# A planned attention and expert kernel: the order of all its tasks is drawn anew, a small load of q moves from ScalarE's queue to GpSimd's, and nine idle products stand where six stood

## The chip, the cores and the metric

The kernel runs on one core of a Trainium2 chip. The metric is device time in microseconds (us) of one execution. It is the median of 3 runs for the kernel before, and one further execution was profiled. TensorE (PE) multiplies matrices and writes to PSUM; VectorE (DVE), ScalarE (ACT) and GpSimd (POOL) work on tiles in SBUF, the first two on PSUM as well; SyncE (SP) issues most transfers.

## The reference

```python
# q, k, v: (4, 8, 1152, 64) float32; w_in (512, 2048), w_out (2048, 512)
q_pool = q.reshape(B, H, S // 2, 2, D).mean(axis=3)
scores = np.matmul(q_pool, k.transpose(0, 1, 3, 2)) / np.sqrt(D)
attn = np.exp(scores - scores.max(-1, keepdims=True))
attn = attn / (attn.sum(-1, keepdims=True) + 1e-09)
x = np.matmul(attn, v).transpose(0, 2, 1, 3).reshape(B * S // 2, H * D)   # (2304, 512)
h = x @ w_in
g = np.where(h > 0, h, np.exp(np.minimum(h, 0)) - 1)
out = g @ w_out
```

## The kernel before

**Units and pairs.** There are four units, one for each batch entry. Each has four pairs of heads, and each pair nine score steps: four tiles of 128 pooled queries for each head, and one step that takes the last 64 queries of both heads. After attention a unit's 576 tokens go through the experts in two groups, of 256 and 320 tokens.

**A score step.** `scores` multiplies q by k into the one PSUM tile `s` (L935 and L941 in float32 for the first two pairs; L956, L961 and L970 in float16 halves for the others). `biggest` on DVE (L985) takes the scaled scores out of `s` into an `ep` tile with the row maximum, and only then can PE write the next scores. `expo` on ACT (L991) makes the exponentials. In the four pairs of the first unit and one later pair PE transposes them (L1067) and they are copied to `pT` (L1077 on ACT or L1080 on DVE); in the other pairs they are divided into a high and a low float16 half (L1036, L1042 or L499, then L1045 on DVE) and transposed by DMA. PE multiplies by v (L1101, L1119).

**Preparing a pair.** `prep` loads q, k and v. The first two pairs are plain: `q_twice` (L655) adds the two rows that are pooled, `flip_turn` (L624) transposes on PE and `flip_out` (L627) copies to `kT` and `qT`. For all later pairs `halves` makes the high half of q and k, and in eleven pairs of v (L676 on ACT, or L499) and then the low half, either on DVE in one pass over two tiles (L693), or on POOL in two passes (L499, then L699).

**Weights.** Thirty-two loads bring w_in and w_out (L805). Each is decoded by three DVE passes (L820, L821, L824; the last two read two tiles), then every 256 columns are split into halves: the high one on ACT (L847), DVE or POOL (L499), the low one on DVE (L850), or on POOL (L499, then L856).

**Experts.** L1229 is the first product and L1310 the second. Between them lie L1242 and L1245 on ACT, `em` on POOL (L1250), ACT (L1255) or DVE (L1260), the join L1265 on DVE, the high half (L1279 or L1287) and the low half (L1283 on POOL or L1291 on DVE). L1326 and L1329 take the result out.

**What sets the order.** Every step is a task added to a plan with the engines that may do it. The table `ORDER` lists all 2,691 tasks with an engine letter each (p, v, a, g, s: PE, DVE, ACT, POOL, SP), and `SLOTS` gives each buffer its place. The kernel emits tasks in that order, so each engine does its own in it; when something starts on the chip follows from the waits alone. The tables come from a search with a replay of the plan. Task costs (such as `Port(...)`, which marks a pass that shares GpSimd's port in the replay) served that search: what the chip executes depends on the tables and the task bodies only. `warm` multiplies the identity by itself into an unused PSUM tile (L760).

Of the kernel before, what the change touches and what calls it, by code (L numbers as in the profile page):

```python
# [32 lines left out]
2s 1s 11p 4a 16v 299s 9p 3a 314s 13v 5a 12a 10a 19v 17p 7p 283s 18a 414p 22s 288s 8a 301v 23s 316v  # L33
370s 294s 415v 14p 15a 427p 285v 20p 21a 428v 429a 0p 437p 435p 289s 431p 27p 34g 416a 31v 290v
319s 422p 438v 28a 404p 372v 32p 29p 439a 432a 423a 417g 405v 35p 25p 26a 406a 36a 291v 460p 461v
440g 441p 442a 321v 37g 42s 38p 40s 433p 30a 462a 434a 33a 450p 451v 443p 296v 418p 407g 436a 496p
497v 452a 419a 444a 293s 410p 420p 421a 45a 292a 39v 453g 458p 459v 408p 409a 6s 313s 309s 463v
411v 430g 41g 483p 484v 44a 359s 445p 446a 456p 468p 469a 304s 412p 473p 457a 295v 466p 474v 298s
498a 499g 467a 46p 447p 315v 47v 311v 413a 475a 519p 284s 448a 476v 297a 464p 454p 504p 48a 520v
449v 465a 49g 424p 485a 52a 300v 455a 505a 303s 509p 500p 510v 306v 481p 317a 487p 482a 502p 477p  # L40
555p 501a 50s 511a 488a 302a 503a 521a 470p 556v 478a 24s 55s 542p 479p 557a 480a 525p 471a 526a
308s 51s 318s 425a 506p 305v 286v 543v 515p 489p 507a 426v 508v 472v 486v 287a 490v 369s 532p 516a
307a 558g 559p 533v 522v 517p 523p 527p 491p 544a 524a 518a 565p 310v 56v 492a 493p 534a 53g 566v
371v 54s 59a 494a 567a 538p 578p 573p 560a 528a 513p 495v 569p 539a 574a 579v 57s 360s 550p 570a
320v 43s 375s 563p 561p 514a 562a 564a 551a 60a 601p 546p 571p 535g 568g 548p 536p 602v 61p 322a
361v 547a 364s 588p 512g 529p 572a 580a 62v 63a 67a 603a 589v 537a 530a 614p 64v 365s 377v 581v
615v 575p 531v 576v 312a 323v 577v 65s 70s 582p 605p 637p 590a 66s 545v 583a 604g 549a 606a 68g
638v 594p 607p 608a 609p 324p 584p 585a 610a 69s 616a 540p 647p 611p 366v 325v 541a 595a 648v 373a
596p 586p 618p 587a 326p 649a 367v 624p 552p 597a 327v 639a 625v 328g 683p 626a 612v 650v 591v 640v
# [36 lines left out]
1996v 1989v 1990g 1974g 1991g 1015v 2034p 1001v 986p 1008a 1016a 1003s 1024p 1009g 1975v 1010a
# [251 lines left out]
def attention_moe_kernel(  # L338
# [69 lines left out]
    def dve(n):  # L408
        return Port(1.08 * n + 75.0)
# [4 lines left out]
    def pol(n):  # L414
        return 0.93 * n + 150.0
# [968 lines left out]
```

## Time and profile before

| | |
|---|---|
| median of 3 runs (lowest, highest) | 743.45 us (743.11, 743.52) |
| the profiled execution | 742.65 us |
| its span, first to last instruction | 740.9 us |
| PE busy | 717.3 us, 97% of the span |
| DVE busy | 625.0 us, 84% |
| ACT busy | 560.6 us, 76% |
| POOL busy | 338.0 us, 46% |

The span is 1.75 us shorter than the execution that it belongs to, and that execution was 0.80 us faster than the median. Busy shares are means over stages with different limits, so the stages below count for more than the table. PE's busy time is the union of pipelined matmuls; it is not a share of its peak.

### The profile page before, as it was taken

What the parts mean: (1) busy time and instruction counts of PE and PEld (TensorE: products, weight loads), DVE (VectorE), ACT (ScalarE), POOL (GpSimd) and SP (SyncE); (2) the same over time, 40 slices, a digit from 0 to 9 for tenths busy, and PEclk for the clock granted to TensorE, in tenths of its full rate; (3) what the DMA queues carried; (4) which work ended last, traced back from release to release, by engine and by line L of the source; (5) the groups of instructions that cost most, each with busy time, mean ns of one, the idle gap of its engine ahead of it and who ended that gap; (6) DMA issues with size and microseconds to landing.
All of it is one profiled execution on the core that took longest, in us unless ns stands there. A gap on an engine that the chain in (4) does not pass through costs nothing.

```text
span 740.9 us, 19632 instructions
## 1 busy us (share of the span) xinstructions
PE 717.3 (97%) x7905; PEld 478.8 (65%) x7905; DVE 625.0 (84%) x1098; ACT 560.6 (76%) x974; POOL 338.0 (46%) x385
## 2 busy tenths in 40 slices
PE   5899998999999999999999999999999999999997
PEld 4577776877565555775676566786665665865753
DVE  6999999999998998879898879899988989875330
ACT  3899997998998887777688766889788564752651
POOL 1322455466626633376465554354646452440430
PEclk9999999999999999999999999999999999999999
DMA  8787834577999998999999999899899998793001
GB/s 304 287 228 251 247 119 105 142 135 160 171 179 207 178 204 169 211 181 174 213 171 208 189 205 181 163 162 209 173 189 194 188 162 137 139 139 64 30 1 36
DMA packets 310971, 126.01 MB, mean 170 GB/s; under 512 B 286304, under 2 KB 288352, under 8 KB 310880
## 3 DMA queue, kind: packets, MB, share of 16 engines
q1 hardware_dynamic: 310432, 124.16, 82.4%
q8 instruction: 62, 1.02, 0.6%
q10 hardware_dynamic: 448, 0.59, 0.2%
q14 instruction: 29, 0.24, 0.1%
HBM read 45.09 MB, written 4.72 MB: 67 GB/s over the span
## 4 chain that ended last, share of the span: by engine, by line
PE 47%; DVE 3%; ACT 2%; issue 1%; DVEq 0%; ACTq 0%
PE r L1310 16%; PE r L1229 14%; PE r L1119 6%; PE s L956 4%; PE s L970 3%; PE r L1101 1%; DVE ep L985 1%; PE r L1067 1%; ACT ep L991 1%; PE s L961 0%; DVE ep L1045 0%; DVE tmp L1265 0%; DVE x L1207 0%; DVE g L1291 0%; ACT hb L1042 0%
## 5 line engine op out<-in xcount | busy, mean ns | idle before, releaser
L991 ACT ACTIVATE ep<-ep,wk 128x1152 f32<-128x1152 f32 x136 | 170.4, 1254 | 45.7 <-DVE ep L985 40.5
L1229 PE MATMUL r<-x,wi 128*128 128x256 f16 (+1 forms) x1536 | 196.6, 286 | 1.5 <-DVE tmp L1265 1.5
L985 DVE TENSOR_SCALAR_CACHE_REDUCE ep<-s,sm 128x1152 f32<-128x1152 f32 x122 | 172.3, 1412 | 13.0 <-PE s L970 9.2
L1229 PEld LDWEIGHTS <-wi 128*128 128x128 f16 x1536 | 147.6, 98 | 43.6 <-issue 6.1
L1310 PE MATMUL r<-wo,g 128*128 128x512 f16 (+1 forms) x864 | 174.9, 380 | 0.1
L1045 DVE SCALAR_TENSOR_TENSOR ep<-ep,wk,hb 128x1152 f16<-128x1152 f32 x99 | 146.0, 1478 | 6.7 <-ACT hb L1042 4.7
L1310 PEld LDWEIGHTS <-g 128*128 128x128 f16 (+1 forms) x864 | 73.3, 100 | 83.8 <-issue 4.7
L956 PE MATMUL s<-kT,qT 128*128 128x512 f16 (+3 forms) x420 | 82.9, 328 | 4.3 <-DVE ep L985 3.3
L1119 PEld LDWEIGHTS <-v 128*64 128x64 f16 x2970 | 77.8, 110 | 11.4 <-issue 10.5
L1119 PE MATMUL r<-pT,v 128*64 128x128 f16 (+1 forms) x2970 | 84.4, 215 | 0.3 <-DVE tmp L1265 0.3
L1283 POOL TENSOR_TENSOR g<-tmp,g 128x320 f16<-128x320 f32 (+1 forms) x61 | 68.1, 1118 | 36.0 <-ACT g L1279 34.4
L499 POOL TENSOR_SCALAR wk<-wk 128x1 f32<-128x1 f32 x68 | 31.2, 459 | 114.3 <-ACT ep L991 93.9
L1042 ACT ACTIVATE hb<-ep,wk 128x1152 f16<-128x1152 f32 x50 | 62.3, 1249 | 17.3 <-POOL wk L1010 8.2
L1036 POOL TENSOR_SCALAR hb<-ep,wk 128x1152 f16<-128x1152 f32 x34 | 44.3, 1303 | 56.6 <-DVE wk L1001 29.6
L1265 DVE SCALAR_TENSOR_TENSOR tmp<-r,tmp 128x320 f32<-128x320 f32 (+1 forms) x96 | 51.5, 551 | 21.5 <-POOL tmp L1250 11.5
L1242 ACT ACTIVATE tmp<-r 128x320 f32<-128x320 f32 (+1 forms) x96 | 45.1, 480 | 23.0 <-PE r L1229 14.7
L1245 ACT ACTIVATE tmp<-tmp,us 128x320 f32<-128x320 f32 (+1 forms) x96 | 57.8, 610 | 2.0 <-DVE us L1184 0.5
L956 PEld LDWEIGHTS <-qT 128*128 128x128 f16 (+1 forms) x420 | 33.9, 100 | 37.4 <-issue 13.7
L970 PE MATMUL s<-kT,qT 64*128 64x512 f16 (+1 forms) x280 | 49.6, 391 | 0.9 <-DVE ep L985 0.9
L1077 ACT ACTIVATE pT<-r 128x384 f32<-128x384 f32 x96 | 43.7, 498 | 8.7 <-PE r L1067 8.4
L1067 PE MATMUL r<-ident,ep 128*128 128x128 f32 x333 | 47.3, 283 | 2.3 <-DVE x L1134 2.3
L1287 POOL TENSOR_SCALAR g<-tmp 128x320 f16<-128x320 f32 (+1 forms) x42 | 28.8, 686 | 39.5 <-DVE tmp L1265 39.5
(163 smaller groups left out, 1044.0 us busy)
## 6 DMA issues: line engine op xcount, KB each, us to landing
v<-in_v_dram SPq DMA_DIRECT2D x16, 576.0 KB, 4.3
k<-in_k_dram SPq DMA_DIRECT2D x15, 576.0 KB, 4.5
g<-in_moe_w_in_dram SPq DMA_DIRECT2D x15, 512.0 KB, 7.2
q<-in_q_dram SPq DMA_DIRECT2D x15, 512.0 KB, 4.3
g<-in_moe_w_out_dram SPq DMA_DIRECT2D x15, 512.0 KB, 5.4
out_dram<-tmp SPq DMA_DIRECT2D x16, 256.0 KB, 3.0
qT<-qT SPq DMA_DIRECT2D x28, 144.0 KB, 3.0
pT<-hb SPq DMA_TRANSPOSE x99, 3.6
```

The source lines that it names most:

```text
L956: nc.tensor.matmul(s.ap[rows, c, 0:n], pr.qT.ap[:, 1 - c % 2, j, rows], keys[h][c], start=first[c], stop=not first[c] and c < 2, skip_grou ...
L970: nc.tensor.matmul(s.ap[rows, c, 0:512], pr.qT.ap[r, c, j, rows], keys[h][c][r], start=first[c], stop=not first[c], skip_group_check=True,)
L985: nc.vector.tensor_scalar(e_(), s.ap.rearrange("p a b -> p (a b)")[:, 0:S], -0.5 / float(D) ** 0.5 if pr.plain else pr.sm.ap[:, 12:13], No ...
L991: nc.scalar.activation(out=e_(), in_=e_(), func=AF.Exp, bias=nm.ap[:, 0:1], scale=-1.0, accum_out=nm.ap[:, 1:2],)
L1042: nc.scalar.activation(out=hb.ap, in_=e_(), func=AF.Copy, scale=nm.ap[:, 1:2])
L1045: nc.vector.scalar_tensor_tensor(out=e16(), in0=e_(), scalar=nm.ap[:, 1:2], in1=hb.ap, op0=ALU.mult, op1=ALU.subtract)
L1067: nc.tensor.transpose(tp.ap[:, c * 128:(c + 1) * 128], e_()[:, (j + c) * 128:(j + c + 1) * 128], ident)
L1119: nc.tensor.matmul(half(h), pr.v16.ap[:, h, order[c], e], p, start=(j + c == 0), stop=(j == 2 and c == NCH - 1), skip_group_check=True,)
L1229: nc.tensor.matmul(hp.ap[:, f * n:(f + 1) * n], w_in16[g][:, a, c, (f0 + f) * 128:(f0 + f + 1) * 128], x16.ap[:, e, c, g0:g0 + n], start=( ...
L1245: nc.scalar.activation(out=en.ap[:, :m], in_=en.ap[:, :m], func=AF.Exp, scale=us.ap[:, 8:9])
L1283: nc.gpsimd.tensor_tensor(out=l, in0=gv, in1=h, op=ALU.subtract)
L1310: nc.tensor.matmul(op.ap[r0:r0 + tn, :], gt[qd].ap[:, a, fi, o:o + tn], w_out16(f // 2)[:, e, f % 2, :], start=(i < 128 // tn), stop=(i >= ...
```

## The change

Four things change. `load_qb`, two transfers of 32 KB for the first pair, is issued by GpSimd instead of ScalarE. `warm` makes nine products, not six. The cost of `halves`' low half of q and v becomes a `Port`, which no engine executes. And both tables are replaced. The diff, with one line of each table:

```diff
 ORDER = """
-2s 1s 11p 4a 16v 299s 9p 3a 314s 13v 5a 12a 10a 19v 17p 7p 283s 18a 414p 22s 288s 8a 301v 23s 316v
+4a 16v 299s 5g 19g 3a 2s 1s 9p 314s 10a 17p 283s 288s 13v 18a 301v 11p 12a 316v 14p 414p 415v 15a
...
 SLOTS = """
-01 00 00 00 03 00 01 00 00 04 00 02 00 00 00 01 00 01 04 04 00 01 01 03 03 00 00 02 00 00 00 02 00
+00 00 00 00 04 00 00 02 00 03 00 01 01 00 00 01 00 01 02 03 00 02 01 04 00 00 00 00 00 00 00 02 00
...
         def load_qb():
             for h in range(2):
-                nc.scalar.dma_start(
+                nc.gpsimd.dma_start(
...
-            tq.append(plan.add("ACT", 900.0, lk - 8.0, load_qb, (), [q32]))
+            tq.append(plan.add("POOL", 2000.0, lk - 8.0, load_qb, (), [q32]))
...
-            t = plan.add("DVE", Port(730.0, 730.0) if j == 1 else dve(n) + 35.0 * (j == 0), kl, f, [h], bufs, ...
+            t = plan.add("DVE", Port(730.0, 730.0) if j == 1 else Port(dve(n) + 35.0 * (j == 0)), kl, f, [h], bufs, ...
...
     def warm():
-        for i in range(6):
+        for i in range(9):
             nc.tensor.matmul(idle.ap[:, 0:128], ident, ident, start=True, stop=True)
...
-    plan.add("PE", 1530.0, -1.0e9, warm, [], [idle])
+    plan.add("PE", 2340.0, -1.0e9, warm, [], [idle])
```

**The start.** SP's queue before, from its first transfer (`k` and `q` are the inputs of the first pair, then of the second; `h` and `g` take raw weights):

```order
L600 DMA k_79<-in_k_dram 128x576 x2
L805 DMA h_88<-in_moe_w_in_dram 128x2x512
L805 DMA g_96<-in_moe_w_in_dram 128x2x512
L805 DMA g_115<-in_moe_w_in_dram 128x2x512
L558 DMA q_123<-in_q_dram 128x2x512
```

SP's queue of the changed kernel from the same place:

```order
L805 DMA h_83<-in_moe_w_in_dram 128x2x512
L600 DMA k_89<-in_k_dram 128x576 x2
L805 DMA g_97<-in_moe_w_in_dram 128x2x512
L805 DMA g_106<-in_moe_w_in_dram 128x2x512
L805 DMA g_108<-in_moe_w_in_dram 128x2x512
L558 DMA q_146<-in_q_dram 128x2x512
```

One weight load now stands ahead of the two loads of k, and a fourth ahead of the next pair's q. POOL's queue of the changed kernel where it makes the identity:

```order
masks.py:197 MEMSET ident 128x128
L593 DMA q_79<-in_q_dram 64x128
masks.py:199 ISA
masks.py:199 AFFINE_SELECT ident<-ident 128x128
L593 DMA q_79<-in_q_dram 64x128
L655 TENSOR_TENSOR kn_81<-q_79 128x128
```

Before, POOL held only the three rows of the identity here; the two L593 stood on ACT's queue and this L655 on DVE's, behind two others. The load q_146 on SP now waits for POOL's L655, which waits for the two L593.

**The splits of w_in.** POOL before, in the first unit, where it makes low halves of k (`kn`) and of w_in (`wi`):

```order
L499 TENSOR_SCALAR k_1117<-k_1117,sm_1139 128x1152
L699 TENSOR_TENSOR kn_1138<-k_1117,kn_1138 128x9x128
L499 TENSOR_SCALAR wk<-wk 128x1
L1013 TENSOR_TENSOR wk<-wk 128x1
L499 TENSOR_SCALAR wi_67<-wi_67,wk 128x1024
L856 TENSOR_TENSOR wi_66<-wi_67,wi_66 128x1024
```

DVE before, beside it:

```order
L985 TENSOR_SCALAR ep_1470,wk<-s_1440,sm_333 128x1152
L1140 COPY x_416<-r_1447 128x128
L1003 TENSOR_SCALAR wk<-wk 128x1
L1004 RECIPROCAL wk<-wk 128x1
L693 SCALAR_TENSOR_TENSOR qn_1214<-q_928,sm_1139,qn_1214 128x9x64
L1134 TENSOR_TENSOR x_416<-r_1447,x_416 128x128
L985 TENSOR_SCALAR ep_1512,wk<-s_1497,sm_333 128x1152
L820 TENSOR_SCALAR tmp_1514<-g_1242 128x512
L821 SCALAR_TENSOR_TENSOR tmp_1514<-g_1242,tmp_1514 128x512
L824 SCALAR_TENSOR_TENSOR wo_1284<-g_1242,tmp_1514 128x512
L1134 TENSOR_TENSOR x_416<-r_1518,x_416 128x128
```

POOL of the changed kernel in the same place:

```order
L699 TENSOR_TENSOR qn_1282<-q_984,qn_1282 128x9x64
L499 TENSOR_SCALAR wi_66<-wi_66,wk 128x1024
L856 TENSOR_TENSOR wi_65<-wi_66,wi_65 128x1024
L499 TENSOR_SCALAR k_1106<-k_1106,sm_1212 128x1152
L699 TENSOR_TENSOR kn_1211<-k_1106,kn_1211 128x9x128
L499 TENSOR_SCALAR wi_67<-wi_67,wk 128x1024
L856 TENSOR_TENSOR wi_66<-wi_67,wi_66 128x1024
```

DVE of the changed kernel beside it:

```order
L985 TENSOR_SCALAR ep_1465,wk<-s_1458,sm_372 128x1152
L1003 TENSOR_SCALAR wk<-wk 128x1
L1004 RECIPROCAL wk<-wk 128x1
L1171 TENSOR_REDUCE us_1473<-x_385 128x1
L985 TENSOR_SCALAR ep_1510,wk<-s_1497,sm_372 128x1152
L820 TENSOR_SCALAR tmp_1545<-g_1158 128x512
L821 SCALAR_TENSOR_TENSOR tmp_1545<-g_1158,tmp_1545 128x512
L824 SCALAR_TENSOR_TENSOR wo_1290<-g_1158,tmp_1545 128x512
L1134 TENSOR_TENSOR x_385<-r_1475,x_385 128x128
```

The low half of this pair's q (qn) has left DVE: POOL makes it by L499 and L699 ahead of the place shown. The decode passes L820, L821 and L824 still stand beside POOL's L499 and L856 on w_in.

**The last expert group.** DVE before, at the start of the last group of 320 tokens:

```order
L1207 SCALAR_TENSOR_TENSOR x_9758<-x_7928,us_10515,x_9758 128x4x320
L1184 TENSOR_SCALAR us_10515<-wk,us_10515 128x1
L499 TENSOR_SCALAR us_10515<-wk,us_10515 128x1 x2
L1265 SCALAR_TENSOR_TENSOR tmp_10646<-r_10632,tmp_10646 128x320
L1265 SCALAR_TENSOR_TENSOR tmp_10683<-r_10669,tmp_10683 128x320
```

DVE of the changed kernel there:

```order
L1207 SCALAR_TENSOR_TENSOR x_9757<-x_7946,us_10592,x_9757 128x4x320
L499 TENSOR_SCALAR us_10592<-wk,us_10592 128x1
L1260 TENSOR_SCALAR tmp_10663<-tmp_10663,us_10592 128x320
L1265 SCALAR_TENSOR_TENSOR tmp_10663<-r_10632,tmp_10663 128x320
L1260 TENSOR_SCALAR tmp_10711<-tmp_10711,us_10592 128x320
L1265 SCALAR_TENSOR_TENSOR tmp_10711<-r_10671,tmp_10711 128x320
```

More of the `em` passes stand on DVE. Over the whole program L1260 goes from 17 to 30, L1291 from 28 to 36 and L1131 from 19 to 30, L1140 from 9 to 2; on POOL L1283 goes from 68 to 60, L1036 from 34 to 28; on ACT L1255 from 47 to 36, L1128 from 36 to 25, L1137 from 16 to 23. PE has the same products but for the three idle ones.

## Rows read from the trace of the kernel before

**Rows 1.** Busy time in stretches (in us): length, engine's busy time (instructions), clock, DMA.

```profile
6.00:20.00 14.00, 12.02 (x61) 8.46 (x61) 12.22 (x20) 6.13 (x11) 2.02 (x3) 1.00 0.99 344
20.00:100.00 80.00, 77.74 (x805) 58.11 (x806) 77.34 (x165) 76.03 (x156) 28.32 (x37) 1.00 0.78 248
100.00:140.00 40.00, 36.48 (x420) 28.71 (x417) 38.62 (x72) 34.48 (x72) 23.12 (x22) 0.96 0.44 113
140.00:240.00 100.00, 96.46 (x1080) 65.88 (x1080) 95.95 (x168) 93.19 (x152) 52.81 (x49) 1.00 0.90 162
240.00:660.00 420.00, 417.70 (x4896) 272.56 (x4890) 372.05 (x618) 315.25 (x521) 212.46 (x242) 1.00 0.99 182
```

**Rows 2.** Timeline of DVE, 113 to 124 us: start, duration, instruction.

```profile
114.00 2.18 DVE L693 SCALAR_TENSOR_TENSOR qn<-q,sm,qn 128x576 f16<-128x576 f32 x1
...
118.10 1.40 DVE L821 SCALAR_TENSOR_TENSOR tmp<-g,tmp 128x512 uint32<-128x512 uint32 x1
119.54 2.50 DVE L824 SCALAR_TENSOR_TENSOR wo<-g,tmp 128x512 uint32<-128x512 uint32 x1
```

**Rows 3.** Timeline of POOL, 111 to 124 us.

```profile
113.19 2.38 POOL L699 TENSOR_TENSOR kn<-k,kn 128x1152 f16<-128x1152 f32 x1
...
117.61 1.36 POOL L499 TENSOR_SCALAR wi<-wi,wk 128x1024 f32<-128x1024 f32 x1 [0.75 <-ACT wi L847]
119.05 2.44 POOL L856 TENSOR_TENSOR wi<-wi,wi 128x1024 f16<-128x1024 f32 x1
```

**Rows 4.** Timeline of PE, 114 to 127 us; in brackets PE's idle time and who ended it.

```profile
122.39 0.52 PE L1067 MATMUL r<-ident,ep 128*128 128x128 f32 x3 [2.26 <-DVE x L1134]
123.63 0.94 PE L956 MATMUL s<-kT,qT 128*128 128x512 f16 x3 [0.72 <-DVE wo L985]
```

**Rows 5.** Busy time in a short stretch, columns as in rows 1.

```profile
123.80:127.30 3.50, 3.50 (x17) 2.55 (x15) 3.00 (x10) 0.65 (x3) 0.00 (x0) 0.51 0.90 200
```

**Rows 6.** The pass L693: ns shortest/median/longest, first and last start.

```profile
L693 DVE SCALAR_TENSOR_TENSOR qn<-q,sm,qn x11: 804/1115/2182, 72.5 to 577.5; 128x576 f16<-128x576 f32 x11
```

**Rows 7.** Timeline of PE, 5.5 to 17 us.

```profile
6.02 1.30 PE L624 MATMUL r<-ident,k 128*128 128x128 f32 x5 [6.02 <-DMA k<-in_k_dram]
...
10.83 0.56 PE L941 MATMUL s<-kT,qT 64*128 64x128 f32 x2
...
14.90 1.50 PE L760 MATMUL r<-ident 128*128 128x128 f32 x12
16.47 0.70 PE L935 MATMUL s<-kT,qT 64*128 64x512 f32 x2
```

**Rows 8.** Timeline of DVE, 4 to 14 us.

```profile
10.65 0.69 DVE L821 SCALAR_TENSOR_TENSOR tmp<-g,tmp 128x512 uint32<-128x512 uint32 x1
11.38 0.69 DVE L824 SCALAR_TENSOR_TENSOR wi<-g,tmp 128x512 uint32<-128x512 uint32 x1
11.99 1.35 DVE L985 TENSOR_SCALAR_CACHE_REDUCE ep<-s 128x1152 f32<-128x1152 f32 x1
```

**Rows 9.** Queues of ACT and SP, 0 to 13 us: start, time in issue.

```profile
1.65 1.16 ACTq L593 DMA_DIRECT2D q<-in_q_dram  x2
...
8.52 0.37 SPq L558 DMA_DIRECT2D q<-in_q_dram  x1
```

**Rows 10.** DVE's groups by shape: count, busy us, mean ns, idle before.

```profile
L985 DVE TENSOR_SCALAR_CACHE_REDUCE ep<-s,sm 128x1152 f32<-128x1152 f32 x122 | 172.3, 1412 | 13.0 <-PE s L970 9.2 <-DMA pT<-ep 1.9 <-PE s L961 0.6
L1045 DVE SCALAR_TENSOR_TENSOR ep<-ep,wk,hb 128x1152 f16<-128x1152 f32 x99 | 146.0, 1478 | 6.7 <-ACT hb L1042 4.7 <-POOL hb L1036 1.4
```

**Rows 11.** The pass L1260: ns shortest/median/longest, first and last start.

```profile
L1260 DVE TENSOR_SCALAR tmp<-tmp,us x17: 368/388/1260, 165.2 to 713.3; 128x320 f32<-128x320 f32 x11, 128x512 f32<-128x512 f32 x6
```

**Rows 12.** Timeline of PE, 302 to 306 us: a score step between first products.

```profile
303.23 0.65 PE L956 MATMUL s<-kT,qT 128*128 128x512 f16 x3
...
304.19 2.03 PE L1229 MATMUL r<-x,wi 128*128 128x256 f16 x17
```

**Rows 13.** PE's waits after 240 us: total us, times, longest.

```profile
PE s L956 <- DVE ep L985: 1.7, 5, 0.6
```

More of the change, by code (lines that the diff above doesn't have):

```diff
@@ L38 @@
[L38 to L49, printed above, removed]
@@ new lines @@
+1199v 185v 190v 2205g 186g 1191v 1200g 172s 1185s 1192a 2121s 1206p 1207v 1208a 1194s 2157g 187v
+1201v 1193v 2158p 2159a 2160a 2113p 2130p 2161v 1209v 2131a 2132a 1210g 2114a 1214p 1215v 1202s
+1186p 2133a 1211v 2162v 1203s 1224p 1195s 193s 1216a 2134v 1217g 1169v 2165p 1225v 2163a 2137p
+1218a 2206g 1219v 191v 1212s 1242p 1204p 176a 1187a 2166a 2167a 2168v 177v 1213s 2164g 2169v 2138a
+2139a 1226a 2170g 1227v 1205v 2140a 1228a 2172p 2115s 1221s 1243v 2186p 1229v 2144p 1220s 1234p
+1230s 1231s 196s 2135g 2179p 2171g 2187a 2188a 2189g 2141v 2136v 1244a 1245v 2145a 2146a 2190v
@@ new lines @@
+2191g 192s 1246a 1235v 2207p 1260p 2173a 2147v 2192v 2148v 1236a 1261v 2180a 1232p 1222p 2174a
+2181a 188s 2182v 1237v 2175v 2149g 2150g 2208a 2209a 2176v 1262a 1263v 2183v 1248s 1252p 1253v
+1247v 1223a 1238a 1240s 2142g 1254a 1239v 2193p 2177g 2235p 1255v 2210g 1233a 2143v 2228p 2211v
+2178v 2184g 2212g 2185g 2236a 2237a 2221p 2238v 2242p 1270p 1249s 1241s 195s 2194a 2195a 2196v
+1264v 1266s 1256v 1257v 2229a 2243p 2230a 1259s 1271v 2231a 2197v 1278p 1272a 198a 1265v 1250p
+1279v 2232v 2239v 2213g 1273g 2198g 1274a 1258s 1280a 1288p 2248p 2249p 194g 197a 199a 200p 1267s
@@ new lines @@
+1747p 2476v 1724g 1725a 1726v 1735s 1736s 2459p 1748v 1727s 1739p 1759a 1728s 1719p 1760g 1761a
+1740v 1737p 2473a 1749a 1763s 1762v 1764s 1785p 1741a 1738a 1742v 1720v 2467a 2468s 2477v 2478p
+2479v 2482a 1786v 1743g 2460p 1750v 2483v 1751g 1765p 1766v 2491p 2480v 1744v 1767a 1745s 1768g
+1746s 2484p 2474v 2492a 2493a 2494v 2475s 1753s 1752v 1769a 1770v 2495v 1787a 1788v 1754s 2485a
+2486a 2487a 1793p 2488v 2496a 2497g 1794v 1795a 2519p 2498p 1789a 1790v 1755p 2489g 1775p 2505p
+1772s 1776v 1771s 2490g 1791s 2499a 2520a 2461a 2521a 1792s 1803p 1756v 2522a 2523v 1796v 1804v
@@ new lines @@
+1773p 1811p 1797v 2481v 1777a 1778g 2533p 1779a 1780v 2506a 2500a 2501g 2507a 2508g 2524g 1812v
+2509v 2510g 1781s 2511v 2502v 1799s 2503g 1798v 2534a 1813a 2535a 1814g 2536g 2504v 1774v 2512p
+2546p 1805a 2513a 2514a 2515g 1806g 2516v 2537v 1782s 1815a 2547p 1800s 1783p 1801p 1817s 1816v
+1807a 2517g 2518v 1809s 1821p 1822v 1823a 1824g 2525g 2538a 2540p 2541p 2526p 2527a 2528a 2529g
+1808v 1825v 1826v 1818s 1802v 2539v 2530v 2531a 1810s 2542p 1827s 1828s 1819p 2462s 1829p 1830a
+2532v 1820a 2543p 1784v 2553v 2552v 2554p 2555v 2558a 2556v 2544a 2548p 2549p 2559v 2581p 2567p
@@ new lines @@
+2557v 2545s 2550a 2582a 2583a 2584v 2585v 2586g 2551s 2587g 2560p 2588p 2574p 2561a 2562a 2563v
+2564v 2568a 2565a 2566v 2569a 2570v 2575a 2576a 2577g 2578v 2589a 2590a 2591v 2592v 2609p 2610a
+2611a 2612g 2613v 2614g 2665p 2602p 2658p 2615v 2593g 2603a 2579a 2580g 2604a 2605a 2606v 2607g
+2616p 2595p 2659a 2660a 2661g 2571v 2662v 2663g 2630p 2594v 2596a 2597a 2598v 2637p 2599v 2572g
+2600g 2573g 2601v 2608v 2638a 2639a 2640g 2641v 2672p 2673p 2631a 2632a 2633g 2634v 2664g 2642g
+2643g 2666a 2617a 2618a 2667a 2619a 2620v 2621g 2668g 2644p 2623p 2669v 2622v 2624a 2625a 2626v
@@ L707, in halves @@
             f, g = lo(dst_l, src, dst_h, j)
-            t = plan.add("DVE", Port(730.0, 730.0) if j == 1 else dve(n) + 35.0 * (j == 0), kl, f, [h], bufs, [("POOL", Port(pol(n), pol2(n)), g)] if CFG["PLP"] else [])
+            t = plan.add("DVE", Port(730.0, 730.0) if j == 1 else Port(dve(n) + 35.0 * (j == 0)), kl, f, [h], bufs, [("POOL", Port(pol(n), pol2(n)), g)] if CFG["PLP"] else [])
             t.pen = CFG["PENH"]
```

266 lines of the change are left out of this document (124 added, 142 removed), and 84 rows, old and new, of the table SLOTS.

## The prediction

> **What bounds the kernel now.** I read the busy time by stretches first [rows 1]. After 240 us PE is never short of work: it is busy 417.70 of 420 us, DVE 372.05, and PE's longest class of waits there is 1.7 us in all [rows 13]. So little can be gained in that part, and something can be lost. From 20 to 240 us PE and DVE are both nearly full: PE's busy time is 77.74 of 80, 36.48 of 40 and 96.46 of 100 us, which leaves 9.3 us idle, and DVE's is 77.34, 38.62 and 95.95, which leaves 8.1. The 40 us from 100 on stand out: PE is idle 3.5 us and its mean granted clock is 0.96.
>
> The timeline shows why. DVE's pass L693 on q takes 2.18 us [rows 2], against 0.80 for the shortest of its kind [rows 6]; it starts at 114.00, while POOL's L699 runs from 113.19 for 2.38 us, and ends soon after it [rows 3]. The decode passes L821 and L824 then take 1.40 and 2.50 us [rows 2] where the first ones of the program take 0.69 [rows 8]; POOL's L499 and L856 run beside them, 117.61 to 118.97 and 119.05 to 121.49 [rows 3]. So a DVE pass that reads two tiles stands still until a POOL operation that began before it is done. The three are late by 1.38, 0.71 and 1.81, in all 3.9 us. PE needs what DVE does next (L1134 frees a PSUM tile, L985 frees `s`) and idles 2.26 and 0.72 us [rows 4]. Right behind that idle time its granted clock is 0.51 for 3.5 us [rows 5], about 1.2 GHz of 2.4, which is worth some 1.7 us of PE's work.
>
> **The change part by part.**
>
> *Start.* PE begins at 6.02 us, when k has landed [rows 7]. A weight load of 512 KB now stands ahead of k on SP's queue; at the 344 GB/s of that stretch [rows 1] it takes 1.5 us, so k's last half lands between 0 and 1.5 us later (ACT's loads of q share the engines in both orders). Thirteen transposes stand ahead of the first score in both. That score's last product ended at 11.39 [rows 7] and L985 could start only at 11.99, because DVE's second decode ran from before until 12.07 [rows 8]; so 0.6 us of the delay is covered. The cost is 0 to +0.9; I take +0.4, because the first four transposes now need only the first half of k.
>
> *Nine idle products.* Six took 1.50 us [rows 7], so nine take 2.25. They follow the second score, as they did. The next score started at 16.47, after DVE had freed `s`; it may now start some 0.7 us later. Nothing waits for that: between DVE's second and third L985 stand three decode passes and a pass of L655, some 2.4 us. I cost it at 0; without that cover it is +0.7. The clock of the first microseconds isn't helped, since the products stand behind two scores.
>
> *q's last part.* Its two issues took 1.16 us on ACT's queue [rows 9], which waits for data then anyway, so nothing is gained there. POOL issues one of them ahead of the identity's last step. PE doesn't need the identity before 6 us, so an issue of up to 4 us is hidden. SP's load of the next q, issued at 8.52 before [rows 9], now waits for POOL's pass on q's last part. I take 0; a late landing is a rival below. How long POOL needs for such an issue no row shows; the nearest is ACT's 0.58 us each, the other end is those 4 us. The Trainium skill (DMA: Bandwidth & Descriptors, "Latency and other measured facts") gives a first byte about 0.4 us later for a transfer issued by GpSimd than for one issued by SP or ACT, so it speaks against this move; by it the sum would stay as it is, because 0.4 us lie inside the same cover. No row of this trace shows a transfer issued by POOL.
>
> *The splits of w_in.* The pass on q that stood still has left DVE for POOL, where it stands ahead of the splits. Between the two score passes of that place DVE has now two small operations and a reduction in place of five operations. If the decode passes then run ahead of L499 and L856, all 3.9 us return to DVE: -3.9.
>
> *More work on DVE.* Counting both orders up to DVE's last split of w_out (the last L850), the changed kernel has 361 rows on DVE where there were 350. The large ones are one L985 more (1.41 us), one L1045 (1.48) [rows 10], three L1080, three L1260, one net pass of L693; five L1140 and one addition of q are gone. With the groups' means, less some 0.06 us by which neighbours overlap, DVE has 5.8 us more to do by then. PE is further on as well at that place: by one score, 303.23 to 304.19 or 0.96 us [rows 12], and ten L1229 of about 0.14 us. So if DVE alone set the pace up to there, this costs 5.8 - 2.4 = +3.4; if DVE's idle 8.1 us take it up, 0. As both engines have about as much idle time (9.3 and 8.1), I take a middle value, +1.5.
>
> *After 240 us.* DVE gets some ten L1260, nine L1291 and ten L1131 more there and two L1140 less; at L1260's median of 0.39 us [rows 11] for each of 27, 10.5 us. DVE's 48 us of idle time [rows 1] cover it: 0. PE changes between kinds of products 527 times instead of 520; the changes that go and come are of many kinds, and I set them at 0.
>
> The sum is 0.4 + 0 + 0 - 3.9 + 1.5 = -2.0. Against the profiled execution (742.65 us) that is 740.6; the median of the runs is 0.80 above it, so I predict **741.4** as a median. A measurement of this kernel can tell about 0.2%, 1.5 us, from no change, so this is just faster.
>
> **The rivals.**
>
> *The same stall returns* (no change). L821, L824, L499 and L856 stand side by side in both orders. What decides is who starts first: before, without L693's lateness, L824 would have begun about 0.2 us ahead of L499's 117.61. The new order gives DVE some 0.6 us more, so if DVE is later than about 0.8 us against ACT's pass that releases L499, the 0.71 and 1.81 come back. Then 743.45 + 0.4 - 1.4 + 1.5, about 744. For it speaks how narrow 0.8 us is, against it that the cause of the lateness is gone.
>
> The Trainium skill (SBUF — State Buffer, "Who interferes with whom") has this as an exclusive lock: whichever of the two engines starts first holds the shared ports for its whole instruction. This trace agrees, with 2.50 us against 0.69. The same section lets some DVE passes with a single source take those ports too, which would put the added L1260 at risk, and the next rival is what that would do here.
>
> *DVE is late for PE in the second half* (slower). The added `em` and low-half passes stand in DVE's queue ahead of the score passes that free `s`. One L1260 took 1.26 us where most take 0.39 [rows 11]. While DVE is 88.6% busy PE idles 0.55 us in 100; at 96% busy it idles 3.5 in 100 [rows 1]. With 10.5 us more DVE stands at 91%, and on the line between the two PE would idle 1.5 us in 100, which costs +4.0: 745.4. It decides the sign from about +2.0 on, that is when DVE passes some 90% with work that can't move. Against it speaks that PE's waits there are now few [rows 13].
>
> *PE gets all of it back* (faster by more). If the stall goes and DVE's extra work falls into idle time, PE regains 3.5 us of waits and the 1.7 us of slow clock: 743.45 + 0.4 - 5.2, about 738.6. More of the 9.3 us could go too, which is what my lower bound allows for.
>
> *POOL's queue holds the start back* (slower). If q's last part lands so late that SP's load of the next q comes more than some 3 us after 8.52, decode and second-pair transposes starve, at 1 us for 1 us: above 745.
>
> **How the numbers follow.** Forecast 0.42 (739.5 to 742.5), the stall returns 0.22, DVE late in the second half 0.18, all of it back 0.13, POOL's queue 0.05. Faster than 741.96: most of the forecast (0.36) and all of it back (0.13), 0.49. Within 1.5 us: 0.05 of the forecast, 0.18 of the returning stall, 0.02 of the late half, 0.25. Slower: 0.26. The range leaves out a tenth at either end: from 736.5, where PE's regained 5.2 us go with some of its waits from 140 to 240 us, to 746.0, just above the late second half.
>
> **What would show it.** Right: L693 on q and the decode passes beside the last POOL splits at 0.8 and 0.69 us, no PE wait over 1 us between 100 and 130 us, no stretch of half clock after the start, and PE's busy share after 240 us as before. Wrong: an L821 or L824 of 1.4 us or more beside L499 or L856; PE's waits for L985 or L1265 above 4 us after 240 us; a first score more than 1 us later; or SP's second load of q issued after 11 us.

## The result, and the profile after

The changed kernel takes 735.11 us (median of 4 runs, 734.75 to 735.23); the kernel before, run beside it, 743.28 (742.83 to 743.52). The ratio is 0.9897, 95% interval 0.9882 to 0.9913: 8.2 us faster where 2.0 were forecast, and below the range's 736.5. The profiled execution took 735.11 us, 7.5 less than the one of before (742.65); its span is 733.3.

Busy time of the changed kernel in stretches (columns as in [rows 1]):

```profile
20.00:100.00 80.00, 77.97 (x779) 57.06 (x777) 76.86 (x159) 76.37 (x159) 31.37 (x41) 1.00 0.77 235
100.00:140.00 40.00, 39.52 (x484) 31.77 (x486) 38.86 (x92) 38.55 (x78) 21.56 (x18) 1.00 0.55 141
140.00:240.00 100.00, 98.34 (x1122) 67.44 (x1120) 97.52 (x172) 90.91 (x150) 54.98 (x52) 1.00 0.90 168
240.00:660.00 420.00, 418.79 (x4956) 273.14 (x4951) 378.67 (x636) 319.25 (x514) 172.91 (x225) 1.00 0.99 180
```

Take PE's idle time (the length less its first busy figure) and compare it with [rows 1]. From 20 to 100 us it was 2.26 and is 2.03; from 100 to 140 it was 3.52 and is 0.48; from 140 to 240, 3.54 and 1.66; from 240 to 660, 2.30 and 1.21. That is 0.2, 3.0, 1.9 and 1.1 us, in all 6.2. The granted clock from 100 to 140 us was 0.96 on the mean and is 1.00, worth another 1.6 us of PE's work. The sum is 7.8, against 7.5 between the profiled executions; the stretches are cut at the same times and not at the same work, so a few tenths are loose. The clock's 1.6 us belong to this execution: the mean granted clock of the kernel before differs from one execution to the next, as the runs beside the experiments show (last paragraph of the run after_again).

The place that the prediction turned on, DVE in the changed kernel (start, duration, instruction):

```profile
111.98 0.69 DVE L821 SCALAR_TENSOR_TENSOR tmp<-g,tmp 128x512 uint32<-128x512 uint32 x1
112.70 0.69 DVE L824 SCALAR_TENSOR_TENSOR wo<-g,tmp 128x512 uint32<-128x512 uint32 x1
117.71 0.69 DVE L821 SCALAR_TENSOR_TENSOR tmp<-g,tmp 128x512 uint32<-128x512 uint32 x1
118.44 0.69 DVE L824 SCALAR_TENSOR_TENSOR wo<-g,tmp 128x512 uint32<-128x512 uint32 x1
```

and POOL beside it:

```profile
106.96 1.28 POOL L699 TENSOR_TENSOR qn<-q,qn 128x576 f16<-128x576 f32 x1
109.43 2.15 POOL L856 TENSOR_TENSOR wi<-wi,wi 128x1024 f16<-128x1024 f32 x1
114.59 2.39 POOL L699 TENSOR_TENSOR kn<-k,kn 128x1152 f16<-128x1152 f32 x1
118.61 1.53 POOL L499 TENSOR_SCALAR wi<-wi,wk 128x1024 f32<-128x1024 f32 x1 [1.62 <-ACT wi L847]
```

The decode passes stand in the gaps: L856 ends at 111.58, L821 starts at 111.98; L699 ends at 116.98, L821 starts at 117.71, and L824 starts 0.17 us ahead of the next L499, which is now the one that waits (1.53 us, where the one of 108.22 us took 1.12). Of the 1.40 and 2.50 us of [rows 2] nothing is left. What PE still waits for from 140 to 240 us, and after 240 (total us, times, longest), against 2.0 us for L985 and 1.5 us for L1265 from 140 to 240 us before, and [rows 13] after 240:

```profile
PE r L1119 <- ACT x L1128: 0.9, 1, 0.9
PE s L956 <- DVE ep L985: 0.4, 1, 0.4
...
PE s L956 <- DVE ep L985: 0.7, 2, 0.5
PE r L1310 <- DVE g L1291: 0.5, 1, 0.5
```

Counted over the whole trace, a DVE instruction's time above the shortest of its line and shape (where over 0.08 us) was 25.0 us before and is 15.9; from 100 to 240 us it fell from 9.3 to 2.7. That is DVE's standing still. In the kernel before all of it, and in the changed one 13.7 of the 15.9 us, lies in passes that began while a POOL operation ran and ended after it.

The start, POOL's two issues of q's last part and SP's second load of q:

```profile
1.27 0.76 POOL L593 DMA_DIRECT2D q<-in_q_dram  x1 [0.34 <-issue]
2.39 0.55 POOL L593 DMA_DIRECT2D q<-in_q_dram  x1
...
8.56 0.37 SPq L558 DMA_DIRECT2D q<-in_q_dram  x1
```

### The profile page after: what moved, and what is told of

Read it like the earlier page. It is cut to its first block, busy times and chain, and to the rows that moved or that the text cites. A ratio compares the mean times of both kernels' runs of the same rounds, so it can differ in the third digit from the quotient of the medians.

```text
span 733.3 us, 19687 instructions
## 1 busy us (share of the span) xinstructions
PE 716.2 (98%) x7911; PEld 479.0 (65%) x7911; DVE 629.3 (86%) x1128; ACT 557.4 (76%) x959; POOL 301.1 (41%) x373
## 3 DMA queue, kind: packets, MB, share of 16 engines
HBM read 45.09 MB, written 4.72 MB: 68 GB/s over the span
## 5 line engine op out<-in xcount | busy, mean ns | idle before, releaser
L985 DVE TENSOR_SCALAR_CACHE_REDUCE ep<-s,sm 128x1152 f32<-128x1152 f32 x123 | 173.7, 1412 | 17.3 <-PE s L970 12.6
L1045 DVE SCALAR_TENSOR_TENSOR ep<-ep,wk,hb 128x1152 f16<-128x1152 f32 x99 | 142.7, 1449 | 5.8 <-ACT hb L1042 3.0
L499 POOL TENSOR_SCALAR wk<-wk 128x1 f32<-128x1 f32 x69 | 24.1, 349 | 165.3 <-ACT ep L991 153.4
L1119 PEld LDWEIGHTS <-v 128*64 128x64 f16 x2970 | 77.7, 110 | 11.6 <-issue 11.1
L1042 ACT ACTIVATE hb<-ep,wk 128x1152 f16<-128x1152 f32 x53 | 66.1, 1249 | 18.3 <-POOL wk L1010 7.8
L1265 DVE SCALAR_TENSOR_TENSOR tmp<-r,tmp 128x320 f32<-128x320 f32 (+1 forms) x96 | 52.0, 552 | 26.9 <-ACT tmp L1255 13.0
L1283 POOL TENSOR_TENSOR g<-tmp,g 128x320 f16<-128x320 f32 (+1 forms) x54 | 54.3, 1011 | 17.4 <-ACT g L1279 16.1
L1036 POOL TENSOR_SCALAR hb<-ep,wk 128x1152 f16<-128x1152 f32 x28 | 38.3, 1367 | 33.0 <-DVE wk L1001 23.2
L1077 ACT ACTIVATE pT<-r 128x384 f32<-128x384 f32 x95 | 42.0, 495 | 5.0 <-PE r L1067 4.6
```

Source lines behind the costliest of these rows:

```text
L985: nc.vector.tensor_scalar(e_(), s.ap.rearrange("p a b -> p (a b)")[:, 0:S], -0.5 / float(D) ** 0.5 if pr.plain else pr.sm.ap[:, 12:13], No ...
L1042: nc.scalar.activation(out=hb.ap, in_=e_(), func=AF.Copy, scale=nm.ap[:, 1:2])
L1045: nc.vector.scalar_tensor_tensor(out=e16(), in0=e_(), scalar=nm.ap[:, 1:2], in1=hb.ap, op0=ALU.mult, op1=ALU.subtract)
L1119: nc.tensor.matmul(half(h), pr.v16.ap[:, h, order[c], e], p, start=(j + c == 0), stop=(j == 2 and c == NCH - 1), skip_group_check=True,)
L1265: nc.vector.scalar_tensor_tensor(out=en.ap[:, :m], in0=hp.ap[:, :m], scalar=2.0 ** -17, in1=en.ap[:, :m], op0=ALU.mult, op1=ALU.max,)
L1283: nc.gpsimd.tensor_tensor(out=l, in0=gv, in1=h, op=ALU.subtract)
```

## The experiments

In what follows "later" or "earlier" by profile is the difference of spans to the changed kernel's 733.3 us or to 740.9 of the kernel before. A token of the order is a step's number and its engine's letter.

**The two edits beside the tables, undone.**

```diff
-                nc.gpsimd.dma_start(
+                nc.scalar.dma_start(
-        for i in range(9):
+        for i in range(6):
```

> The changed kernel with two of its edits undone: q's last part is issued by ACT again, and six idle products follow the second score in place of nine. If the gain is the new order's (the waits theory: DVE's passes that read two tiles no longer stand still behind POOL), the time stays at 735.1 us within 0.7. If these two edits carry a part of the gain, it is 736 to 738 or more. First transposes on PE at about 7.2 us in either case, since the load of w_in ahead of k on SP's queue is left.

Measured 736.69 us (735.41 to 740.06, ratio to before 0.9925, 0.9901 to 0.9949); three of six runs lie at 735.4 to 735.6, the profiled one among them with a span of 733.7 us, 0.4 more. The other three reach from 737.8 to 740.1 at a mean granted clock of 1.000 and have no profile, so what held them is open. By the median, 1.6 us above the changed kernel, the second branch of the expectation came; by the three fastest and the profiled span the two edits carry some tenths. The run is also not quite the old start: ACT issues the two L593 between its two L585, where the kernel before issued them behind both [rows 9], and the DVE pass L655 that needs the second L585 starts at 8.64 us, where it starts at 6.31 in the changed kernel. So the tables carry most of the gain, and what the two edits are worth is known to 0.4 to 1.6 us only.

**The kernel before with one step moved.**

```diff
-357v ... 732v 740v 681v 719v 80v
+357v ... 80v 732v 740v 681v 719v
```

> The kernel before with one step moved: the pass L693 on q that took 2.18 us at 114.00 is issued one score pass earlier on DVE, ahead of POOL's L699. Waits theory: it takes 0.8 us there, L821 and L824 run ahead of L499 and L856 at 0.69 us each, PE's waits of 2.26 and 0.72 us and the half clock behind them go, and the time is 738 to 739.5. The prediction's pricing (DVE's 3.9 us alone) gives 739.5. If the two decode passes still start behind L499, only 1.4 us come back: 742. If PE's idle time at 117 to 127 us had another cause (ACT's chain or the order of PE's own steps), 743.3.

Measured 739.69 us (738.9 to 741.76) beside 743.09 for before: ratio 0.9957 (0.9942 to 0.9973), 3.2 us faster. DVE, POOL, and the stretch from 100 to 140 us of this kernel (its profiled execution began some 2.4 us later, which shifts the times):

```profile
114.40 1.78 DVE L693 SCALAR_TENSOR_TENSOR qn<-q,sm,qn 128x576 f16<-128x576 f32 x1
120.76 0.69 DVE L821 SCALAR_TENSOR_TENSOR tmp<-g,tmp 128x512 uint32<-128x512 uint32 x1
121.48 1.49 DVE L824 SCALAR_TENSOR_TENSOR wo<-g,tmp 128x512 uint32<-128x512 uint32 x1
```

```profile
113.86 1.71 POOL L499 TENSOR_SCALAR k<-k,sm 128x1152 f32<-128x1152 f32 x1 [2.71 <-ACT kn L676]
121.04 1.40 POOL L499 TENSOR_SCALAR wi<-wi,wk 128x1024 f32<-128x1024 f32 x1 [1.72 <-ACT wi L847]
```

```profile
100.00:140.00 40.00, 37.83 (x463) 30.22 (x459) 38.68 (x79) 37.45 (x77) 24.74 (x24) 1.00 0.45 122
```

The step met another POOL operation, L499 on k, so only a part of the standing still is gone: 1.78, 0.69 and 1.49 us where [rows 2] have 2.18, 1.40 and 2.50, which is 2.1 of the 3.9 us. PE's idle time fell by 1.35 us and the clock no longer falls there, 1.00 in place of 0.96. With the clock's 1.6 us that is 3.0 us, for one token of 2691. The clock's part is not the same in every execution. At a mean granted clock of 0.999 or 1.000 this kernel takes 738.9 to 739.4 us and the kernel before 740.3 to 740.8: 1.4 us, about the idle time alone, and less than the 2.1 us that DVE got back. But with this step moved (here and in b_two_moves below) 9 of 19 executions reach 0.999, and of the kernel before 9 of 63. This kernel's own profiled execution lost clock at another place: the granted clock was 0.83 in its first 20 us, and 1.00 in every stretch that was read from 20 to 140 us.

```profile
0.00:20.00 20.00, 11.63 (x45) 8.39 (x46) 12.03 (x22) 6.70 (x11) 1.95 (x7) 0.83 0.88 310
```

**A price for DVE's time: 22 added reductions from 130 to 240 us.**

```diff
+            if j in PADS:
+                self.pad()
...
+    def pad():
+        nc.vector.tensor_reduce(out=spare, in_=ident, axis=AX.X, op=ALU.max)
```

> The changed kernel with 22 reductions of the identity added on DVE, some 0.25 us each, 5.5 us in all, spread over 130 to 240 us; nothing reads them. It prices a microsecond of DVE work in that stretch. The prediction's upper bound (DVE sets the pace) gives 735.1 + 5.5 = 740.6; the prediction's middle value (some 40% of it) 737.3; if DVE's work there is free, 735.1 within 0.5.

Measured 740.04 us (738.74 to 740.63), 0.9957 of before (0.9941 to 0.9973). The added passes (ns shortest/median/longest, first and last start) here and in the next kernel:

```profile
L1361 DVE TENSOR_REDUCE wk<-ident x22: 267/277/280, 132.1 to 242.6; 128x1 f32<-128x128 f32 x22
```

They are 6.1 us by their length, some 4.8 if neighbours overlap by 0.06; the span is 5.0 longer. From 130 to 240 us added work costs 0.8 to 1 us for 1 us. Part of that price is indirect: the passes that now come later stand still 4.8 us there where it was 2.7, so counted with this the price is some 0.7.

**The same after 270 us**, 40 of them at other places of the order.

```diff
-557, 577, 612, 640, 653, 674, 694, 707, 722, 748, 773, 794, 808, 822, 836, 852, 872, 898, 919,
+1117, 1150, 1174, 1204, 1238, 1269, 1306, 1324, 1351, 1377, 1409, 1435, 1463, 1499, 1522, 1555,
```

> The changed kernel with 40 of the same reductions spread over 270 to 600 us, some 10 us in all. The prediction set work of this size there at nothing: 735.1 within 0.5. The rival that DVE comes late for PE in the second half gives +4 us for it: 739.

```profile
L1362 DVE TENSOR_REDUCE wk<-ident x40: 268/277/282, 273.8 to 601.1; 128x1 f32<-128x128 f32 x40
```

Measured 738.84 us (738.16 to 739.75), the span 4.0 longer for 11.1 us of work: 0.4 us for 1 us. DVE's idle time there covers only a part.

**POOL made to stand beside DVE: four of its subtractions twice.** Four steps (49, 84, 333, 337) issue their `tensor_tensor` two times.

```diff
+            self.times = 2 if t.n in (49, 84, 333, 337) else 1
...
+            for _ in range(plan.times):
+                nc.gpsimd.tensor_tensor(out=to()[:, 1], in0=x(), in1=to()[:, 0], op=ALU.subtract)
```

> The changed kernel with four of POOL's subtractions issued twice (L699 of two pairs, 1.3 and 2.4 us, and L856 at 99.51 and 109.43 us, 2.1 us each); the second one writes the same values, and POOL has idle time behind three of the four. DVE's decode passes L821 now begin beside the second ones. Waits theory: each of those L821 stands still until POOL is done, 1.0 to 1.8 us, some 6 us of DVE's time in all; since a microsecond of DVE costs about 0.9 us in the stretch that was priced (130 to 240 us), PE is 4 to 6 us later by 140 us: 739 to 741, and more if PE's clock falls again. If POOL's work beside DVE is not what holds DVE, L821 stays at 0.69 us and the time at 735.1 within 1.

Measured 742.27 us (741.04 to 743.86): ratio to before 0.9995 (0.9981 to 1.0009). The whole gain is gone. The lines of this kernel are two or three further down (L822 is L820, L859 is L856). DVE, then POOL, then two short stretches:

```profile
102.97 2.37 DVE L822 TENSOR_SCALAR tmp<-g 128x512 uint32<-128x512 uint32 x1
115.12 2.51 DVE L823 SCALAR_TENSOR_TENSOR tmp<-g,tmp 128x512 uint32<-128x512 uint32 x1
117.66 1.59 DVE L826 SCALAR_TENSOR_TENSOR wo<-g,tmp 128x512 uint32<-128x512 uint32 x1
```

```profile
100.70 4.35 POOL L859 TENSOR_TENSOR wi<-wi,wi 128x1024 f16<-128x1024 f32 x2
112.56 4.52 POOL L859 TENSOR_TENSOR wi<-wi,wi 128x1024 f16<-128x1024 f32 x2
117.06 1.66 POOL L500 TENSOR_SCALAR k<-k,sm 128x1152 f32<-128x1152 f32 x1
```

```profile
120.00:123.50 3.50, 2.86 (x22) 2.39 (x22) 3.40 (x8) 2.27 (x5) 3.42 (x2) 0.76 0.01 2
123.50:127.00 3.50, 3.50 (x32) 2.71 (x31) 3.43 (x5) 3.50 (x8) 2.48 (x3) 0.75 0.52 113
```

The diff shows one of the two loops; L699 has the same. Each of these DVE passes ends soon after POOL's: L822 at 105.34, POOL's pair at 105.05; L823 at 117.63, the pair at 117.08; L826 at 119.25, L500 at 118.72. DVE stands still 7.1 us more by 140 us, PE idles 4.72 us from 100 to 140 where it idled 0.48, its longest wait (2.6 us) for DVE's score pass and another of 1.5 us for ACT's copy to `pT`, and the clock behind it, from 120 to 127 us, falls to 0.76 and 0.75. Eleven of this kernel's twelve executions have a mean granted clock of 0.997 or 0.998, where the changed kernel's ten on record have 0.999 or 1.000. POOL is idle 14.7 of these 40 us even so, so most of the loss comes from its place beside DVE; what the later results of the doubled operations cost by themselves is not separated.

**The same from 163 to 218 us**, with passes L1283.

```diff
+            self.times = {1845: 3, 1859: 3, 1887: 3, 1928: 4}.get(t.n, 1)
...
-                        nc.gpsimd.tensor_tensor(out=l, in0=gv, in1=h, op=ALU.subtract)
+                        for _ in range(plan.times):
+                            nc.gpsimd.tensor_tensor(out=l, in0=gv, in1=h, op=ALU.subtract)
```

> The changed kernel with four of POOL's passes L1283 between 163 and 218 us issued three times (three of them) or four times (one), in all nine more, 9.3 us of POOL's time; the repeats write the same values. DVE's L1045 at 165.2 and 178.4, L499 at 195.2 and L1260, L499 and L850 at 218.6 to 219.6 then begin beside a repeat. Waits theory: they stand still for 3 to 6 us in all, and PE is 0.8 to 1 us later for each of these by 240 us: 738 to 741. If the waits of DVE in this stretch do not reach PE, 735.1 within 1, and the second part of the gain (140 to 240 us) has another cause.

Measured 739.43 us (738.95 to 740.1), 0.9965 of before (0.9952 to 0.9978). Lines are one or two further down:

```profile
163.89 1.05 DVE L1180 TENSOR_TENSOR us<-us 128x1 f32<-128x1 f32 x1
165.24 2.14 DVE L1046 SCALAR_TENSOR_TENSOR ep<-ep,wk,hb 128x1152 f16<-128x1152 f32 x1
178.70 2.31 DVE L1046 SCALAR_TENSOR_TENSOR ep<-ep,wk,hb 128x1152 f16<-128x1152 f32 x1
```

```profile
162.53 3.64 POOL L1285 TENSOR_TENSOR g<-tmp,g 128x512 f16<-128x512 f32 x3
175.84 3.94 POOL L1285 TENSOR_TENSOR g<-tmp,g 128x512 f16<-128x512 f32 x3 [0.76 <-ACT g L1280]
```

```profile
140.00:240.00 100.00, 94.09 (x1027) 63.87 (x1024) 97.23 (x164) 88.12 (x146) 61.85 (x57) 1.00 0.85 159
```

DVE stands still 7.2 us from 140 to 240 us where it was 2.7, and PE idles 5.91 where it was 1.66: 4.5 and 4.3 us. DVE's waits there reach PE nearly one for one.

**The changed kernel once more, beside that run.**

> The changed kernel once more, unchanged, on the chip of the run beside it: 735.1 within 1.5, and 7 to 8 us below the kernel before; PE's idle time from 100 to 140 us 0.5 us, and the clock at 1.00 there in its profile.

Measured 735.61 us (733.93 to 736.31), before 741.75 (740.32 to 743.76): ratio 0.9912 (0.9896 to 0.9928), 6.1 us. PE idles 0.48 us from 100 to 140 us again, and the clock is 1.00 there. The difference to 8.2 us lies in the kernel before, whose time goes with its mean granted clock: of its 63 executions beside these experiments the nine at 1.000 took 740.3 to 740.8 us, the 17 at 0.992 to 0.994 took 743.5 to 745.0. The profiled one, at 0.998, has its low clock behind the stall; where the others have theirs no profile shows, and it need not be there (b_q_early had it at the start). At 1.000 the changed kernel's first four executions (734.8 to 735.2) lie some 5.4 us below those nine. So of the 8.2 us some 3 come and go with the clock, of which the profiles place 1.6 behind the stall.

**Another stall of the kernel before, at 175 us**, with the first move kept:

```diff
-855v 1914v 878p 1851a 1863a 1864v 864a 840p 856s 1852g 1929p 879v
+1914v 878p 1851a 1863a 1864v 864a 840p 856s 1852g 1929p 879v 855v
```

> The kernel before with two steps moved: the pass L693 on q one score pass earlier, as in the run before, and at 175 us the pass L1045 behind L1207, L1265 and the score pass, so that L1207 starts ahead of POOL's L1283 (in the kernel before it took 2.45 us beside it, and PE then waited 1.04 us for L1265). Waits theory: L1207 takes 1.54 us, the wait of 1.04 us goes and PE is 1.0 us earlier from 180 us on, beside the 3.1 us of the first move by 130 us: 738.5 to 739.5. If L1207's length was not what PE waited for, nothing more than the first move's gain: 739.7.

Measured 739.87 us (739.0 to 741.49), 0.9971 of before (0.9959 to 0.9984): no more than the first move.

```profile
174.19 1.54 DVE L1207 SCALAR_TENSOR_TENSOR x<-x,us,x 128x1280 f16<-128x1280 f32 x1
182.43 1.42 DVE L985 TENSOR_SCALAR_CACHE_REDUCE ep<-s,sm 128x1152 f32<-128x1152 f32 x1 [0.90 <-DMA pT<-ep]
```

```profile
183.90 0.38 PE L956 MATMUL s<-kT,qT 128*128 128x512 f16 x1 [1.02 <-DVE ep L985]
```

In the kernel before the pass L1207 stood here:

```profile
176.50 2.45 DVE L1207 SCALAR_TENSOR_TENSOR x<-x,us,x 128x1280 f16<-128x1280 f32 x1
```

Moved, L1207 took 1.54 us as expected and PE's wait for L1265 went; but L1045 now came later, so did the transfer that reads its `ep`, and the next score pass waited 0.90 us for that buffer. A stall cured by hand came back one step on, so taking DVE's standing still out of a place need not gain anything there.

**The added L1260 taken back from DVE.**

```diff
-1891v ... 1960v ... 1925v ... 1974v ... 2002v ... 2106v
+1891a ... 1960a ... 1925a ... 1974g ... 2002a ... 2106g
...
```

> The changed kernel with 25 of its 30 passes L1260 on DVE given back to the engine that had them before (15 to ACT, 10 to POOL); their places in the order stay. The prediction set this added DVE work after 240 us at nothing: 735.1 within 1. At the price that the 40 added reductions showed there (4.4 us for 11 us of them), 10 us less on DVE gives 731 to 733, if ACT and POOL are not late with them. If the passes then come late on ACT or hold DVE up from POOL, 735 to 738.

Measured 743.24 us (742.68 to 745.77), 1.0013 of before (1.0000 to 1.0027): the span is 7.6 us longer than the changed kernel's, with DVE busy 7.7 us less in all. PE idles 3.67 us from 140 to 240 us and 5.93 from 240 to 660, where it idled 1.66 and 1.21, and DVE's L1265 waits 7.3 us for ACT's L1255 after 240 us where it waited 2.8:

```profile
DVE tmp L1265 <- ACT tmp L1255: 7.3, 8, 3.2
```

These steps' engine and their places in the order belong together: at the same places on ACT they come later, and L1265, which frees PE's `r`, waits for them.

**Engines alone, and order alone.** The order of before with the changed kernel's engines in all 392 steps that differ (load_qb left out), and the reverse. The first few of the former:

```diff
-19v ... 34g ... 31v ... 39v ... 453g ... 459v ... 463v
+19g ... 34v ... 31g ... 39a ... 453v ... 459a ... 463g
...
```

Of the first:

> The kernel before with its order kept and only the choice of engine taken from the changed kernel, for each of the 392 steps that have another engine there. If the choice of engines carries the gain, 736 to 738. If it is where the steps stand against each other (waits theory: a pass that reads two tiles beside POOL or not beside it), the choice alone, in an order that was not made for it, gives no gain: 742 to 748.

Of the second:

> The reverse: the order of the changed kernel with the engines that the kernel before chose, 392 steps. By the waits theory the passes fall beside POOL's operations again, DVE's lost time is back near 25 us or above (15.9 in the changed kernel) and the time is 741 to 748. If the order of the steps by itself carries the gain, 735 to 737.

Measured 835.66 us (834.15 to 836.4; ratio 1.1245, 1.1223 to 1.1268) and 836.86 (835.08 to 838.8; ratio 1.1265, 1.1239 to 1.1290): both far outside what was expected. PE's longest class of waits in each (the first kernel, then the second):

```profile
PE s L956 <- DVE ep L985: 19.9, 19, 5.0
```

```profile
PE s L956 <- DVE ep L985: 31.9, 25, 3.9
```

DVE's standing still is some 31 and 40 us. That is 15 and 24 more than in the changed kernel, and not 100, so most of the loss is something else, probably steps that come late on engines for which their place was not made; that was not tried. Neither half of the tables is worth anything without the other; these two runs don't tell more.

**The changed kernel with k first on SP's queue, and L1128 ahead of L1042 on ACT.**

```diff
-4a 16v 299s 5g 19g 3a 2s 1s
+4a 16v 2s 1s 299s 5g 19g 3a
...
-872a 841a
+841a 872a
```

> The changed kernel with k's two loads ahead of the first load of w_in on SP's queue again, and ACT's pass L1128 at 177.49 us ahead of L1042, behind which it stood while PE waited 0.85 us for it. Start: PE begins near 6.0 us in place of 7.2, and 0.3 to 1.0 us of it are left at 95 us, since DVE waits 1.5 us for the first score there. ACT's pass: PE's wait of 0.85 us goes, but if DVE sets the pace from 130 to 240 us little of it is left at 240 us. 734 to 735.1; slower only if w_in's later landing holds the first decode up, which would show as a DVE wait before L820.

Measured 736.32 us (734.51 to 739.39; ratio 0.9929, 0.9903 to 0.9954), span 734.0. Nothing is gained in the whole. PE at both:

```profile
4.91 1.09 PE L624 MATMUL r<-ident,k 128*128 128x128 f32 x4 [4.91 <-DMA k<-in_k_dram]
...
13.31 1.13 PE L935 MATMUL s<-kT,qT 64*128 64x512 f32 x4 [3.17 <-DVE ep L985]
```

```profile
184.07 0.68 PE L956 MATMUL s<-kT,qT 128*64 128x512 f16 x6 [1.01 <-DVE ep L985]
```

PE begins at 4.91 and then waits 3.17 us for the first score pass, which stands behind decode passes whose weights landed later. The second scores still start 0.9 us earlier (13.31, where the changed kernel has 14.18). But the granted clock of the first 20 us is 0.91 here (the line below) and 1.00 in the changed kernel's profile, and the means of the six executions are 0.994 to 0.999, where the changed kernel's are 0.999 and 1.000. So the order of the loads is not priced apart from the clock.

```profile
0.00:20.00 20.00, 11.80 (x56) 8.79 (x57) 11.14 (x20) 6.54 (x10) 3.37 (x11) 0.91 0.94 335
```

The wait of 0.85 us for L1128 went and one of 1.01 us for DVE came 6 us on. No version here beats the changed kernel.

## Why the prediction was wrong

The mechanism was right at the place that the prediction looked at, and three terms of the sum were not, one of them with the wrong sign. By the prediction's steps:

- *Start, +0.4.* The first score pass on DVE starts at 12.66 us where it was 11.99 ([rows 8] end there): +0.7, and PE's idle time from 20 to 100 us is 0.2 less, so about +0.5 is left, the size forecast. With k first again PE's second scores came 0.9 us earlier and nothing was gained in the end, at a lower granted clock; what the load ahead of k is worth alone stays open.
- *Idle products and q's last part, 0.* Right within what was measured: a_old_start's span differs by 0.4, its median by 1.6 for a reason that is open. POOL's issues took 0.76 and 0.55 us beside ACT's 1.16 for both [rows 9], SP's second load of q stands at 8.56 after 8.52. The Trainium skill's later first byte for GpSimd (DMA: Bandwidth & Descriptors, "Latency and other measured facts") did stay inside that cover; no row here shows the 0.4 us by itself.
- *The splits of w_in, -3.9.* DVE got all of it back, at that place. The step is too small because it counts DVE's time alone: the idle time and the clock behind it, which the prediction worked out as 3.5 and 1.7 us, are what PE lost, and they were put into a rival at 0.13. Measured between the profiled executions, 3.0 and 1.6: -4.6. b_q_early and a_twice show that PE's idle time goes and comes with DVE's standing still. The clock follows in a_twice (11 of 12 executions at 0.998 or less) and in part in b_q_early, where a larger share of executions keeps 0.999 or more; nine executions of the kernel before kept 1.000 all the same.
- *More work on DVE, +1.5.* This step failed most. Its price was not too high: a microsecond of work added to DVE from 130 to 240 us costs PE 0.8 to 1, nearer the prediction's +3.4 than its middle value. What it left out is that the rest of DVE's standing still, outside the one place, would change as well. It fell from 5.0 to 2.7 us between 140 and 240 us, and PE's idle time by 1.9, with more work on DVE (97.52 us busy where it was 95.95). Places of that sort stood in the trace of before and were not looked at one by one: L1207 at 176.50 took 2.45 us beside POOL's L1283, where it took 1.54 moved ahead of it. That the standing still that went is the cause of these 1.9 us is inferred, and not shown: a_again_mid puts 4.5 us of it back and PE idles 4.3 us more, but b_two_moves took one such place out by hand and gained nothing.
- *After 240 us, 0.* PE idles 1.1 us less there. The cover that the prediction named is partial: added work costs 0.4 us for 1. The change's own L1260 took the place of passes on ACT and POOL; put back there at the same places of the order they make the span 7.6 us longer, which prices the steps and their places together. Which part of the 1.1 us is which step's was not tried.

Of the rivals, the returning stall and the late second half did not come, and POOL's queue did not hold the start. The one nearest, *PE gets all of it back*, gave 738.6; it lacks the 3.0 us of PE's idle time after 140 us. All ten executions of the changed kernel lie below the range's 736.5, so the miss is not one run's luck. But the sum also started from executions of the kernel before that stand 2 to 3 us above its nine at a clock of 1.000, and none of its terms gave that back. The signs that the text named came as the forecast had them: 0.69 us for the decode passes, no PE wait over 1 us from 100 to 130 us (0.5 in all from 100 to 140), no half clock there, 418.79 us of 420 busy after 240, and 0.7 us of waits for L985. The Trainium skill's exclusive lock (SBUF — State Buffer, "Who interferes with whom") is borne out by a_twice, in which each delayed pass shown ends 0.3 to 0.6 us after POOL's operation.

## What to carry to other kernels

Cost a removed stall as PE loses it, in idle time and, where the trace shows it behind the stall, slow clock, and not as the engine that stood still loses it. When a whole order is made anew against one kind of wait, list every instance of that wait in the old trace (instructions of one line and shape that took longer than the shortest) and price them all, knowing that one taken out may come back one step on. Price added work by what the engine's time is worth in that stretch, which a few idle passes in it measure.

## What was not expected of the hardware

- A DVE pass with one source stands still too: L820 on 512 words took 2.37 us beside POOL's pair, where it takes 0.42 (the row of a_twice at 102.97). The Trainium skill (SBUF — State Buffer, "Who interferes with whom") names some passes with one source that do; the trace agrees for this one, with the 1.95 us between the two.
- A short pass waits too: L1179 of the changed kernel, over 128x1, took 1.05 us beside POOL's L1283 (a_again_mid at 163.89, there L1180), and 0.16 us in the median of its eight in the changed kernel.
- In one case a DVE pass that had waited was not passed over by POOL's next operation: L823 of a_twice, issued at 115.12 while the second of the pair ran, ended at 117.63, 0.55 us after the pair, and POOL's L500, which started at 117.06, took 1.66 us where the median of its like is 1.24.
- POOL waits as well: its L499 at 118.61 took 1.53 us beside L824, and 1.12 us at 108.22.
